# Decode attention over 65,536 keys on one core: engine programs written by hand with their own semaphores, TensorE in a hardware loop, a fixed buffer for each tile

## The chip, the cores and the metric

The kernel runs on one core of a Trainium2 chip. Its time is the device time of one execution in microseconds (us), the median of three runs. The profile comes from one further execution; its times count from the first instruction of the program, and the stretch from there to the last instruction is called the span.

Five engines work side by side, each through its own list of instructions: TensorE (PE, with PEld for its weight loads), VectorE (DVE), ScalarE (ACT), GpSimd (POOL) and SyncE (SP). Here SP does nothing but issue the large loads, ACT issues the load of the queries and the stores. A load is cut over 16 DMA engines, each of which works through its share of the loads in the order in which they were issued; such a list is called a ring below.

## What is computed

One query token with 32 heads attends over 65,536 keys; four query heads share one of eight key/value heads ("a head" below is one of these eight, numbered 0 to 7).

```
B, Hq, Hkv, Sq, Sk, D = 1, 32, 8, 1, 65536, 128      # q, k, v in bf16
k = jnp.repeat(k, rep, axis=1)                        # rep = 4
v = jnp.repeat(v, rep, axis=1)
scores = jnp.einsum("bhqd,bhkd->bhqk", q, k) * scale  # scale = D ** -0.5
p = _softmax(scores, axis=-1)
return jnp.einsum("bhqk,bhkd->bhqd", p, v)
```

Keys and values are 2 x 8 x 65,536 x 128 x 2 bytes = 268.4 MB, each read once. Everything else is small.

## The kernel before

**Tiles.** A head's K and its V come in two tiles each (`s` = 0 and 1, called first and second half), [128 partitions, 256 keys, 128] in bf16, 8.39 MB. A tile lies in one of three buffers of the pool `iopool` (L61, L115), which are handed out in turn: tile n goes where tile n-3 lay, whatever the two hold. The order of the tiles is the order of the loop at L298: K0 first, K0 second, K1 first, V0 first, K1 second, V0 second, K2 first, V1 first and so on; at the end ... K7 second, V6 second, V7 first, V7 second. The very first tile comes in four pieces and the very last in seven (128, 64, 32, 16, 8, 4, 4 keys per partition), so that work can begin early and little is left when the last byte lands.

**Work on a K tile** (`k_step`, L124). DVE transposes the tile in place in four parts (L135); behind each part PE runs 16 matmuls (L141) against the queries, which lie spread out in `wq`. Each half of a tile fills one PSUM bank `sc` with scores, four banks a head; DVE takes each bank's maximum (L148).

**Softmax** (`softmax`, L150). A chain of small steps: maximum over the four banks (L152), a PE transpose (L154), maximum per query head (L156), scaling (L160), a matmul that spreads it (L166), a copy (L168). ACT then computes the exponentials of the four banks (L172) with their sums, and DVE transposes them into `ET` (L181).

**Work on a V tile** (`v_stream`, L187): 64 matmuls (L197) of `ET` against V into `psum_o`. Behind a head's second V tile, `pick` (L205) keeps the right blocks with a mask in four DVE steps (L213, L215), and for each pair of heads `finish` (L231) sums over partitions with a matmul against `sel` (L234), sums the exponentials (L222, L226), inverts (L228) and multiplies (L237). Two stores carry heads 0 to 3 and 4 to 6 away.

**The end** (`finish_last`, L250). The last tile's pieces are used as they land: 48 matmuls of the usual kind for 128 and 64 keys, then 56 that put V on the weight side and give the transposed result `psum_oT` (L282), and eight single ones that give it straight (L268). The transposed part is copied (L286), turned back by a PE transpose (L289), scaled (L292) and added to the straight part (L293); a store follows (L296).

**Order and waits.** The Tile framework lays the five lists out, puts in the semaphores and holds a load back until its buffer's last reader is done. SP's list holds the loads alone, so one that waits holds back all behind it. On PE the scheduler put the matmuls of V6's second half right behind those of K7's second half, ahead of the small softmax matmuls of head 7.

Of the kernel before, what the change touches and what calls it, by code (L numbers as in the profile page):

```python
# [8 lines left out]
ALU = mybir.AluOpType  # L9
ACT = mybir.ActivationFunctionType  # L10
AX = mybir.AxisListType


NT = 256
NB = 128
NW = 16

LATE = (64, 120, 124)
# [3 lines left out]
def kernel(  # L22
# [16 lines left out]

    nc = tc.nc  # L40
# [7 lines left out]
    KT = R // NT  # L48
# [3 lines left out]
    assert W * HPG == 32 and NU == 4 and U == 2  # L52
    SCALE = float(D) ** -0.5

# [3 lines left out]
    const = ctx.enter_context(tc.tile_pool(name="const", bufs=1))  # L58
    opool = ctx.enter_context(tc.tile_pool(name="opool", bufs=1))
    stats = ctx.enter_context(tc.tile_pool(name="stats", bufs=1))  # L60
    iopool = ctx.enter_context(tc.tile_pool(name="iopool", bufs=3))  # L61
    epool = ctx.enter_context(tc.tile_pool(name="epool", bufs=1))
    psc = ctx.enter_context(tc.tile_pool(name="psc", bufs=5, space=bass.MemoryType.PSUM))
    psm = ctx.enter_context(tc.tile_pool(name="psm", bufs=1, space=bass.MemoryType.PSUM))
    pso = ctx.enter_context(tc.tile_pool(name="pso", bufs=2, space=bass.MemoryType.PSUM))


    qn = epool.tile([P, D], bf16, name="qn", tag="E_g")
    for a in range(4):
        nc.scalar.dma_start(out=qn[32 * a:32 * a + 32, :], in_=q[0, :, 0, :])  # L70


    WX = P + 32
    wq = const.tile([P, 4 * WX], bf16)
    nc.vector.memset(wq[:, :], 0.0)
    ident = const.tile([P, P], fp32)
    make_identity(nc, ident[:, :])

    sel = const.tile([P, HPG], fp32)
    nc.vector.tensor_reduce(  # L80
        out=sel[:, :], in_=ident[:, :].rearrange("p (x h) -> p h x", h=HPG), axis=AX.X, op=ALU.max
    )
    blk = const.tile([P, W], fp32)
    nc.vector.tensor_reduce(
        out=blk[:, :], in_=ident[:, :].rearrange("p (j w h) -> p w j h", w=W, h=HPG), axis=AX.XY, op=ALU.max
    )

    mask = const.tile([P, 4], fp32)
    nc.gpsimd.tensor_copy(out=mask[0:64, :], in_=blk[0:64, 0:4])
    nc.gpsimd.tensor_copy(out=mask[64:128, :], in_=blk[64:128, 4:8])  # L90
    one = const.tile([1, 1], fp32)
    nc.gpsimd.memset(one[:, :], 1.0)
    o_out = const.tile([HPG, Hkv - 1, D], bf16)
    lsum_all = const.tile([P, Hkv, NU], fp32)
    qx = const.tile([P, D], bf16)
    nc.vector.transpose(out=qx[:, :].bitcast(fp32), in_=qn[:, :].bitcast(fp32))  # L96

    qv = qx[:, :].rearrange("p (b h r) -> p b r h", b=2, r=2)

    def queries(g):  # L100
        eng = nc.vector if g == 0 else nc.gpsimd
        wv = wq[:, :].rearrange("p (b r x) -> p b r x", b=2, r=2)
        for a in range(4):
            qd = slice(32 * a, 32 * a + 32)
            eng.tensor_copy(  # L105
                out=wv[qd, :, :, 32 * a + 28:32 * a + 28 + HPG],
                in_=qv[qd, :, :, g * HPG:(g + 1) * HPG],
            )

    queries(0)  # L110

    sc_tiles, mx_tiles, ET_tiles, o_tiles, sum_tiles = {}, {}, {}, {}, {}

    def load(x, name, g, s, pieces=(NT,)):
        t = iopool.tile([P, NT, D], bf16, name=name, tag="io", align_bytes=2048)  # L115
        src = x[0, g].rearrange("(p n) d -> p n d", p=P)
        n = 0
        for step in pieces:
            n0 = s * NT + n
            nc.sync.dma_start(out=t[:, n:n + step, :], in_=src[:, n0:n0 + step, :])  # L120
            n += step
        return t

    def k_step(g, s, kn):  # L124
        if s == 0:
            mx_tiles[g] = stats.tile([P, NU], fp32, name="mx4")
        for u in range(U):
            nu = s * U + u
            sc = psc.tile([P, 4 * P], fp32, name="sc")
            sc_tiles[g, nu] = sc  # L130
            for w in range(W):
                n0 = u * NB + w * NW
                if w % 4 == 0:
                    groups = kn[:, n0:n0 + 4 * NW, :].rearrange("p n d -> p (n d)").bitcast(fp32)
                    nc.vector.transpose(out=groups, in_=groups)  # L135
                kv = kn[:, n0:n0 + NW, :].rearrange("p n (b i r) -> p n b i r", b=2, r=2)
                for b in range(2):
                    for r in range(2):
                        bp = 2 * b + r
                        at = bp * WX + 28 - 4 * w  # L140
                        nc.tensor.matmul(  # L141
                            out=sc[:, :],
                            lhsT=wq[:, at:at + P],
                            rhs=kv[:, :, b, :, r],
                            start=(w == 0 and bp == 0),
                            stop=(w == W - 1 and bp == 3),
                        )
            nc.vector.tensor_reduce(out=mx_tiles[g][:, nu:nu + 1], in_=sc[:, :], axis=AX.X, op=ALU.max)  # L148

    def softmax(g):  # L150
        mx = stats.tile([P, 1], fp32, name="mx")
        nc.vector.tensor_reduce(out=mx[:, :], in_=mx_tiles[g][:, :], axis=AX.X, op=ALU.max)  # L152
        psum_t = psm.tile([1, P], fp32, name="psum_t", tag="misc")
        nc.tensor.transpose(out=psum_t[:, :], in_=mx[:, :], identity=ident[:, :])  # L154
        m4 = stats.tile([1, HPG], fp32, name="m4")
        nc.vector.tensor_reduce(  # L156
            out=m4[:, :], in_=psum_t[:, :].rearrange("o (x h) -> o h x", h=HPG), axis=AX.X, op=ALU.max
        )
        mrow = stats.tile([1, P], fp32, name="mrow", tag="row")
        nc.vector.tensor_scalar_mul(  # L160
            out=mrow[:, :].rearrange("o (x h) -> o x h", h=HPG),
            in0=m4[:, :].unsqueeze(1).broadcast_to([1, 32, HPG]),
            scalar1=-SCALE,
        )
        psum_b = psm.tile([P, 1], fp32, name="psum_b", tag="misc")
        nc.tensor.matmul(out=psum_b[:, :], lhsT=mrow[:, :], rhs=one[:, :], start=True, stop=True)  # L166
        nmb = stats.tile([P, 1], fp32, name="nmb")
        nc.vector.tensor_copy(out=nmb[:, :], in_=psum_b[:, :])  # L168

        E_g = epool.tile([P, NU, 4 * P], bf16, name="E_g", tag="E_g")  # L170
        for nu in range(NU):
            nc.scalar.activation(  # L172
                out=E_g[:, nu, :],
                in_=sc_tiles[g, nu][:, :],
                func=ACT.Exp,
                bias=nmb[:, 0:1],
                scale=SCALE,
                accum_out=lsum_all[:, g, nu:nu + 1],
            )
        ET = epool.tile([P, NU, NW, 32], bf16, name="ET")  # L180
        nc.vector.transpose(  # L181
            out=ET[:, :, :, :].rearrange("p s c x -> p (s c x)"),
            in_=E_g[:, :, :].rearrange("p s x -> p (s x)"),
        )
        ET_tiles[g] = ET

    def v_stream(g, s, vb, halves, last):  # L187

        if s == 0:
            o_tiles[g] = pso.tile([P, 4, D], fp32, name="psum_o")  # L190
        for u in range(U):
            vv = vb[:, u * NB:(u + 1) * NB, :].rearrange("p (w c) d -> p w c d", c=NW)
            n = min(2, halves - 2 * u)
            for x in range(n):
                for c in range(NW):
                    j = 2 * x + c % 2
                    nc.tensor.matmul(  # L197
                        out=o_tiles[g][32 * j:32 * j + 32, :, :],
                        lhsT=ET_tiles[g][:, s * U + u, c, :],
                        rhs=vv[:, 4 * x:4 * x + 4, c, :],  # L200
                        start=(s == 0 and u == 0 and c < 2),
                        stop=(last and c >= NW - 2 and 2 * u + x >= halves - 2),
                    )

    def pick(g):  # L205

        if g % 2 == 0 or g == Hkv - 1:
            o_pair = opool.tile([P, 2, D], fp32, name="o_pair")
        else:
            o_pair = sum_tiles[g - 1]  # L210
        sum_tiles[g] = o_pair
        o = o_pair[:, g % 2, :]
        nc.vector.tensor_scalar_mul(out=o, in0=o_tiles[g][:, 0, :], scalar1=mask[:, 0:1])  # L213
        for x in range(1, 4):
            nc.vector.scalar_tensor_tensor(  # L215
                out=o, in0=o_tiles[g][:, x, :], scalar=mask[:, x:x + 1], in1=o, op0=ALU.mult, op1=ALU.add
            )

    def sums(g0, n):

# [131 lines left out]
```

## Time and profile before

| | |
|---|---|
| median of 3 runs | 629.92 us (629.47 to 630.63) |
| profiled execution | 629.52 us, span 627.7 us, granted TensorE clock 0.798 |
| bytes from HBM | 268.47 MB, 428 GB/s over the span |
| PE busy | 346.2 us (55%), 2141 matmuls |
| DVE busy | 339.2 us (54%), 193 instructions |
| ACT busy | 23.6 us (4%) |
| POOL busy | 6.4 us (1%) |
| K turned, L135 | 64 x 4414 ns, 279.0 us |
| K matmuls, L141 | 1024, 260.1 us busy |
| V matmuls, L197 | 1008, 76.6 us busy |

A row of the profile's groups gives the line, the engine, the operation, the busy time of the group, the mean duration of one and the time for which the engine stood idle just before them, with what ended it. An engine's idle time costs nothing by itself; what matters is which work ends last, and whether the DMA engines ever stand still.

### The profile page before, as it was taken

What the parts mean: (1) busy time and instruction counts of PE and PEld (TensorE: products, weight loads), DVE (VectorE), ACT (ScalarE), POOL (GpSimd) and SP (SyncE); (2) the same over time, 40 slices, a digit from 0 to 9 for tenths busy, and PEclk for the clock granted to TensorE, in tenths of its full rate; (3) what the DMA queues carried; (4) which work ended last, traced back from release to release, by engine and by line L of the source; (5) the groups of instructions that cost most, each with busy time, mean ns of one, the idle gap of its engine ahead of it and who ended that gap; (6) DMA issues with size and microseconds to landing.
All of it is one profiled execution on the core that took longest, in us unless ns stands there. A gap on an engine that the chain in (4) does not pass through costs nothing.

```text
span 627.7 us, 4762 instructions
## 1 busy us (share of the span) xinstructions
PE 346.2 (55%) x2141; PEld 145.4 (23%) x2141; DVE 339.2 (54%) x193; ACT 23.6 (4%) x65; POOL 6.4 (1%) x37
## 2 busy tenths in 40 slices
PE   0829582827539084480844808448193581926744
PEld 0313230313214032130311303113041230412312
DVE  3938855739165490654907549074580845709411
ACT  0000100010000100010000010001000001000010
POOL 0000000000000000000000000000000000000000
PEclk9979795967859678596875958758687695876959
DMA  9999999999999999999999999999999999999996
GB/s 369 435 468 402 464 405 460 409 456 413 452 418 448 422 443 427 439 430 435 434 431 439 431 435 434 431 439 427 443 426 444 422 448 418 448 418 452 410 423 281
DMA packets 6161, 268.79 MB, mean 428 GB/s; under 512 B 892, under 2 KB 1148, under 8 KB 1404
## 3 DMA queue, kind: packets, MB, share of 16 engines
q1 hardware_dynamic: 5904, 268.44, 99.0%
q8 instruction: 17, 0.28, 0.2%
q10 hardware_dynamic: 236, 0.04, 0.0%
q14 instruction: 4, 0.03, 0.0%
HBM read 268.47 MB, written 0.01 MB: 428 GB/s over the span
## 4 chain that ended last, share of the span: by engine, by line
DMA 41%; DVE 23%; PE 23%; another core or an unknown queue 11%; ACT 1%; issue 1%; SPq 0%; DVEq 0%; ACTq 0%
DMA kn<-in_k_dram 35%; DVE kn L135 20%; PE sc L141 17%; DMA vb<-in_v_dram 5%; PE psum_o L197 5%; ACT E_g L172 1%; DMA qn<-in_q_dram 1%; DVE o_pair L215 1%; DVE mx L148 1%; DVE ET L181 0%; PE psum_b L166 0%; PE psum_f L234 0%; DVE m L156 0%; PE psum_t L154 0%
## 5 line engine op out<-in xcount | busy, mean ns | idle before, releaser
L141 PE MATMUL sc<-kn,wq 128*128 128x512 bf16 x1024 | 260.1, 415 | 242.9 <-DVE kn L135 242.6
L135 DVE STREAM_TRANSPOSE kn<-kn 128x4096 f32<-128x4096 f32 x64 | 279.0, 4414 | 149.2 <-DMA kn<-in_k_dram 149.2
L141 PEld LDWEIGHTS <-wq 128*128 128x128 bf16 x1024 | 104.9, 103 | 395.9 <-issue 173.2
L197 PE MATMUL psum_o<-vb,ET 128*32 128x512 bf16 x1008 | 76.6, 394 | 11.1 <-DMA vb<-in_v_dram 11.1
L148 DVE TENSOR_REDUCE mx<-sc 128x1 f32<-128x512 f32 x32 | 21.5, 673 | 53.0 <-PE sc L141 53.0
L197 PEld LDWEIGHTS <-ET 128*32 128x32 bf16 x1008 | 34.7, 99 | 50.4 <-issue 19.1
L172 ACT ACTIVATE E_g<-sc,nmb 128x512 bf16<-128x512 f32 x32 | 21.6, 686 | 564.4 <-DVE nmb L168 564.4
L213 DVE TENSOR_SCALAR o_pair<-psum_o,mask 128x128 f32<-128x128 f32 x8 | 2.8, 350 | 49.2 <-PE psum_o L197 49.2
L181 DVE STREAM_TRANSPOSE ET<-E_g 128x2048 bf16<-128x2048 bf16 x8 | 18.4, 2302 | 11.7 <-ACT E_g L172 11.7
L105 POOL COPY wq<-qx 32x16 bf16<-32x16 bf16 x28 | 5.3, 190 | 493.0 <-PE sc L141 491.8
L215 DVE SCALAR_TENSOR_TENSOR o_pair<-psum_o,mask,o_pair 128x128 f32<-128x128 f32 x24 | 8.3, 345 | 0.5
L172 ACT ACTIVATION_READ_ACCUMULATOR E_g<-sc,nmb 128x1 f32 x32 | 6.5, 203 | 0.0
L166 PE MATMUL psum_b<-one,mrow 1*128 1x1 f32 x16 | 2.9, 245 | 5.7 <-DVE mrow L160 5.7
L234 PE MATMUL psum_f<-o_pair,sel 128*4 128x256 f32 (+1 forms) x8 | 2.2, 352 | 6.4 <-DVE o_pair L215 6.4
L96 DVE STREAM_TRANSPOSE qx<-qn 128x64 f32<-128x64 f32 x1 | 0.2, 245 | 9.7 <-DMA qn<-in_q_dram 9.7
L154 PE MATMUL psum_t<-ident,mx 128*1 128x128 f32 x8 | 2.2, 270 | 5.9 <-DVE mx L152 2.9
L222 PE MATMUL psum_l<-lsum_all,sel 128*4 128x8 f32 (+1 forms) x10 | 1.0, 170 | 6.3 <-ACT E_g L172 6.3
L166 PEld LDWEIGHTS psum_b<-one,mrow 1*128 1x128 f32 x16 | 2.4, 186 | 7.0 <-PE psum_t L154 7.0
L156 DVE TENSOR_REDUCE m<-psum_t 1x4 f32<-1x128 f32 x8 | 2.2, 278 | 3.0 <-PE psum_t L154 3.0
L168 DVE COPY nmb<-psum_b 128x1 f32<-128x1 f32 x8 | 1.3, 158 | 4.3 <-PE psum_b L166 4.3
L237 DVE TENSOR_TENSOR o_out<-psum_f,rl 4x256 bf16<-4x256 f32 (+1 forms) x4 | 1.5, 378 | 2.5 <-PE psum_f L234 2.5
L154 PEld LDWEIGHTS psum_t<-ident,mx 128*1 128x1 f32 x8 | 0.6, 79 | 9.6 <-DVE mx L152 4.4
(31 smaller groups left out, 15.7 us busy)
## 6 DMA issues: line engine op xcount, KB each, us to landing
kn<-in_k_dram SPq DMA_DIRECT2D x4, 2048.0 KB, 12.0
vb<-in_v_dram SPq DMA_DIRECT2D x1, 4096.0 KB, 27.1
vb<-in_v_dram SPq DMA_DIRECT2D x1, 2048.0 KB, 31.5
vb<-in_v_dram SPq DMA_DIRECT2D x1, 1024.0 KB
vb<-in_v_dram SPq DMA_DIRECT2D x1, 512.0 KB, 34.3
vb<-in_v_dram SPq DMA_DIRECT2D x1, 256.0 KB, 34.5
vb<-in_v_dram SPq DMA_DIRECT2D x2, 128.0 KB, 26.9
kn<-in_k_dram SPq DMA_DIRECT2D x15, 51.6
```

Source lines behind the costliest of these rows:

```text
L105: eng.tensor_copy(out=wv[qd, :, :, 32 * a + 28:32 * a + 28 + HPG], in_=qv[qd, :, :, g * HPG:(g + 1) * HPG],)
L135: nc.vector.transpose(out=groups, in_=groups)
L141: nc.tensor.matmul(out=sc[:, :], lhsT=wq[:, at:at + P], rhs=kv[:, :, b, :, r], start=(w == 0 and bp == 0), stop=(w == W - 1 and bp == 3),)
L148: nc.vector.tensor_reduce(out=mx_tiles[g][:, nu:nu + 1], in_=sc[:, :], axis=AX.X, op=ALU.max)
L154: nc.tensor.transpose(out=psum_t[:, :], in_=mx[:, :], identity=ident[:, :])
L156: nc.vector.tensor_reduce(out=m4[:, :], in_=psum_t[:, :].rearrange("o (x h) -> o h x", h=HPG), axis=AX.X, op=ALU.max)
L166: nc.tensor.matmul(out=psum_b[:, :], lhsT=mrow[:, :], rhs=one[:, :], start=True, stop=True)
L172: nc.scalar.activation(out=E_g[:, nu, :], in_=sc_tiles[g, nu][:, :], func=ACT.Exp, bias=nmb[:, 0:1], scale=SCALE, accum_out=lsum_all[:, g, ...
L181: nc.vector.transpose(out=ET[:, :, :, :].rearrange("p s c x -> p (s c x)"), in_=E_g[:, :, :].rearrange("p s x -> p (s x)"),)
L197: nc.tensor.matmul(out=o_tiles[g][32 * j:32 * j + 32, :, :], lhsT=ET_tiles[g][:, s * U + u, c, :], rhs=vv[:, 4 * x:4 * x + 4, c, :], start ...
L213: nc.vector.tensor_scalar_mul(out=o, in0=o_tiles[g][:, 0, :], scalar1=mask[:, 0:1])
L215: nc.vector.scalar_tensor_tensor(out=o, in0=o_tiles[g][:, x, :], scalar=mask[:, x:x + 1], in1=o, op0=ALU.mult, op1=ALU.add)
```

## The change

Only the schedule, the buffers and the handling of sums change; tile sizes and the large matmuls and transposes stay.

- The kernel writes each engine's list itself inside one critical section, with some twenty semaphores of its own. The engines meet once more at its start and at its end.
- The three buffers are fixed: `A` for first halves of K, `Bb` for second halves of K, `C` for all V tiles. The seven pieces of V7's second half go into `A`. The order of the loads stays as it was. SP waits for the reader of the buffer ahead of each load (L131 to L142).
- PE runs its steps for heads 1 to 7 with the values of heads 0 to 6 as a loop of seven passes (L381); ahead of it stand K0 and its softmax, behind it V7. Inside a pass the order is: K first half, V first half, K second half, softmax matmuls (`maxima`), V second half, sum. Semaphores that PE waits for are counted down again (`take`).
- On DVE, `bank_max(0)` stands between the third and the fourth part of a tile in all heads, and `ET` of a head is made after `pick` of the head before.
- The sums of the exponentials become a 129th column of `o_sb` (L240), so that one matmul of 4 x 129 gives result and sum of a head (L392); each head is finished by itself (L282, L284). `mask` is made on DVE, ahead of the first K tile, instead of on POOL. At the end the transposed part is added by a product with the identity into the same PSUM bank as the straight part (L427), in place of transpose, scaling and addition.

```diff
+    io = [sb(f"io{b}", [P, NT, D], bf16, 2048) for b in "ABC"]
...
+    section = tc.tile_critical()
+    ctx.enter_context(section)
+
+    sy = nc.sync
+    for i in range(4):
+        n0 = i * NT // 4
+        sy.dma_start(out=A[:, n0:n0 + NT // 4, :], in_=k_src[0][:, n0:n0 + NT // 4, :]).then_inc(s_part[i], 16)
+    sy.dma_start(out=Bb[:, :, :], in_=k_src[0][:, NT:R, :]).then_inc(s_kb, 16)
+    for g in range(1, Hkv):
+        sy.wait_ge(s_bank, NU * (g - 1) + U)
+        sy.dma_start(out=A[:, :, :], in_=k_src[g][:, 0:NT, :]).then_inc(s_ka, 16)
+        if g > 1:
+            sy.wait_ge(s_vd, 2 * (g - 1))
+        sy.dma_start(out=C[:, :, :], in_=v_src[g - 1][:, 0:NT, :]).then_inc(s_v, 16)
+        sy.wait_ge(s_bank, NU * g)
+        sy.dma_start(out=Bb[:, :, :], in_=k_src[g][:, NT:R, :]).then_inc(s_kb, 16)
+        sy.wait_ge(s_vd, 2 * (g - 1) + 1)
+        sy.dma_start(out=C[:, :, :], in_=v_src[g - 1][:, NT:R, :]).then_inc(s_v, 16)
+    sy.wait_ge(s_vd, 2 * L)
+    sy.dma_start(out=C[:, :, :], in_=v_src[L][:, 0:NT, :]).then_inc(s_v, 16)
+    sy.wait_ge(s_bank, NU * L + U)
+    n = 0
+    for i, step in enumerate(PARTS):
+        sy.dma_start(out=A[:, n:n + step, :], in_=v_src[L][:, NT + n:NT + n + step, :]).then_inc(s_late[i], 16)
+        n += step
...
+    for g in range(Hkv):
+        turn_k(g, 0)
+        at = turn_k(g, 1)
+        ve.wait_ge(s_d, at)
+        ve.tensor_reduce(out=mx[:, :], in_=mx4[:, :], axis=AX.X, op=ALU.max).then_inc(s_m, 1)
...
+        if g > 0:
+            pick(g - 1)
+        ve.wait_ge(s_x, g + 1)
...
+        ve.transpose(
+            out=ET[:, :, :, :].rearrange("p s c x -> p (s c x)"), in_=E_g[:, :, :].rearrange("p s x -> p (s x)")
+        ).then_inc(s_et, 1)
+        if g > 0:
+            after_pe()
+            at = done(ve.reciprocal(out=rl[:, :], in_=psum_f[:, D:D + 1]))
+            ve.wait_ge(s_d, at)
+            ve.tensor_scalar_mul(out=o_out[:, g - 1, :], in0=psum_f[:, 0:D], scalar1=rl[:, 0:1]).then_inc(s_o, 1)
...
+    def take(s, n=1):
+        te.wait_ge(s, n).then_inc(s, -n)
...
+    def maxima():
+        take(s_m)
+        te.transpose(out=psum_t[:, :], in_=mx[:, :], identity=ident[:, :]).then_inc(s_pe, 1)
+        take(s_m)
+        te.matmul(out=psum_b[:, :], lhsT=mrow[:, :], rhs=one[:, :], start=True, stop=True).then_inc(s_pe, 1)
...
+    k_tile(0)
+    k_tile(1)
+    maxima()
+
+    with nc.Fori(0, L, 1, engines=(PE,)):
+        take(s_et)
+        take(s_wq, 4)
+        k_tile(0)
+        take(s_v, 16)
+        v_tile(0, C)
+        k_tile(1)
+        maxima()
+        take(s_v, 16)
+        v_tile(1, C)
+        take(s_pick)
+        te.matmul(out=psum_f[:, :], lhsT=sel[:, :], rhs=o_sb[:, :], start=True, stop=True).then_inc(s_pe, 1)
+
+    take(s_et)
+    te.matmul(out=psum_b[0:HPG, :], lhsT=sel[:, :], rhs=lcol[:, :], start=True, stop=True).then_inc(s_pe, 1)
+    take(s_v, 16)
+    v_tile(0, C)
+    v_tile(1, A, 3)
...
+    single(n2, n3)
+    take(s_m)
+    te.matmul(out=psum_l, lhsT=oT[:, :], rhs=ident[:, :], start=False, stop=False)
+    single(n3, NB).then_inc(s_pe, 1)
```

`s_bank` counts finished score banks (four a head), `s_vd` finished V tiles (two a head, raised by the tile's last matmul), `L` is 7. `k_tile(s)` is the 64 matmuls of one K tile with a `take(s_k)` ahead of each 16; `v_tile(s, t)` the 64 of one V tile.

## The prediction

> **What bounds the kernel now.** I looked first at the page's slices and queues, to see whether any engine or the transfers are full.
>
> ```profile
> DMA  9999999999999999999999999999999999999996
> ...
> q1 hardware_dynamic: 5904, 268.44, 99.0%
> q8 instruction: 17, 0.28, 0.2%
> ```
>
> The load queue fills 99.0% of the 16 DMA engines' time, and no slice but the last is below 9 tenths; PE and DVE are at 55% and 54%. The trace's single packets say the same: a ring moves 64 KB in 2.418 us, an 8.39 MB tile lands every 19.32 us, and between 3 and 620 us no ring rests. So the time is a start, 268.4 MB at full rate, and an end; nothing on the other engines counts unless it makes the rings run dry. Whether that can happen is read from SP's timeline, which says when a load enters the rings (start us, duration):
>
> ```profile
> 476.17 0.33 SPq L120 DMA_DIRECT2D kn<-in_k_dram  x1
> 510.19 0.33 SPq L120 DMA_DIRECT2D vb<-in_v_dram  x1
> 514.68 0.33 SPq L120 DMA_DIRECT2D kn<-in_k_dram  x1
> 548.95 56.39 SPq L120 DMA_DIRECT2D vb<-in_v_dram  x9
> ```
>
> These are K7 first, V6 first, K7 second, and then V6 second with all of V7. K7 second entered at 514.68 and had landed at 566.46: two tiles always lie ahead of the one issued. The third view is the chain of waits around the same place (start us, us, what), with one earlier head for the softmax steps:
>
> ```profile
> 122.51 0.70 DVE mx L148
> ...
> 124.42 0.35 PE psum_b L166 x2
> 124.77 3.63 PE psum_o L197 x57
> ...
> 435.39 5.20 PE psum_o L197 x55
> ...
> 510.16 4.50 PE psum_o L197 x64
> ...
> 566.46 17.43 DVE kn L135 x4
> 583.89 0.04 issue
> 583.93 3.66 PE sc L141 x16
> 587.59 0.02 issue
> 587.61 0.33 SPq L120
> ...
> 624.59 0.22 PE psum_t L289
> 624.80 0.03 issue
> 624.83 0.35 DVE o_t L292
> ...
> 625.27 0.34 DVE o_out L293
> ```
>
> A landed K tile takes 17.43 us of DVE and 3.66 of PE, the softmax steps up to L166 2.26 us (122.51 to 124.77), a V tile 4.50 us of PE.
>
> **The change, part by part.** *1. The order of loads against the fixed buffers (L131 to L142).* In the middle this costs nothing. If a first K half lands at 0, V first lands at 19.3, K second at 38.6, V second at 57.9, the next at 77.3. K first is used up at 17.43 + 0.65 (`bank_max(0)`) + 3.66 = 21.8, V first at 26.3; the load that needs C then has to enter by 38.6 less the 2.1 us below: 10 us spare. K second is used up at 60.4, its softmax steps end at 62.6, V second at 67.1; needed by 75.2: 8 us spare. DVE's `pick` and `ET` behind it (0.1 + 4 x 0.35 + 2.31) end at 71 and the next K first lands at 77.3, so the later `ET` is covered too; without that cover it would push the next K tile by 4 us.
>
> At the end the order has no K tile between V6 second and V7 first, and both lie in C. `sy.wait_ge(s_vd, 14)` (L140) stands ahead of all eight remaining loads, 8.39 MB and the seven pieces, although A has long been free. That wait ends when V6's second half is used up, and PE reaches that only behind K7's second half and its softmax matmuls: 566.46 + 17.43 + 0.65 + 0.04 + 3.66 + 2.26 + 4.50 + 0.05 = 595.0. The restart of empty rings: the first load was issued at 0.74, its first packet starts at 1.75, and its 2.1 MB were down by 7.35 to 7.88, which is 4.84 us at full rate behind 2.5 to 3.0. I take 2.1 us from issue to full flow (bounds 1.0 and 2.3). So V7 flows from 597.1. Before, the slowest ring passed from V6 to V7 at 585.3. **Gap: 11.8 us**, and it is bare: behind it the same bytes, the same pieces and the same end follow. PE's clock is a bound: 64 matmuls behind the softmax steps took 4.5 us at 124.77 and 6.1 at 435.39, where windows show a granted clock of 0.50; +1.6 at most.
> [...]
>
> *2. The first head.* Here K0 second and K1 first are neighbours. K0 second lands at 42.23 and is used up at 64.0; softmax to L168 66.6, four exponentials 2.8, `ET` 2.31: 71.8 (before, one part of K1 was turned in that hole). K1 first then takes to 93.6, V0 first to 98.1. V0 second enters there, and the load ahead of it, K1 second, ran out at 99.3 on the first ring and 100.95 on the last. With 2.1 us of restart the last ring is dry for nothing; bounds 0 and +1.5; I take 0.
>
> *3. The loop.* PE's program now is some 600 recorded instructions, about 1170 with the weight loads, against 4282 profiled. Before, the profile shows 17 instruction packets, one for each 250 instructions. In the packet records each holds its ring up by 1.35 us (a ring's landing went from 60.8 to 62.3 behind the first), and they go round eight rings, so these are 2.7 us late by the end: 563.0 against 566.0 for K7 second. If the program's 4.6 blocks come once, no ring has more than one: **-1.35 us**. Bounds: -2.7 (none) and 0 (one packet for each 250 executed, since about as many are executed as before). The jump back itself falls where PE waits anyway: in the terms of part 1 the sum matmul ends about 69.5 and the next K tile's first part is turned at 77.3 + 4.4 = 81.7, so 12 us hide it.
>
> *4. DVE and POOL.* Per head a 0.1 us sum is added and the small steps lose their partners; DVE stands idle 17 us ahead of K7's second half alone, and 149.2 us in all before L135 for DMA. Making `mask` ahead of the first tile delays it by 0.3 us, and A's next load enters at 35.7 instead of 35.4, needed by 39. Both nothing.
>
> *5. The end.* Before: transpose 0.27, o_t 0.35, o_out 0.34. Now an f32 product (two passes, 0.38 as at L275), four single matmuls and one 0.35 step. The singles run behind it instead of beside o_t; that gives 0 (bounds -0.3 and +0.2).
>
> *6. Entry and exit.* One more meeting of the engines at each end. The span's last DMA ends at 626.5 and the span at 627.7, so such a meeting is under 1.2 us. I take 0.3 together (bounds 0 and 1.0).
>
> Sum: 11.8 - 1.35 + 0.3 = +10.75 on the profiled execution's span of 627.7, with 1.8 us around it: 629.52 + 10.75 = 640.3. That execution lies 0.4 below the median of the runs, so **640.7 us**.
>
> **The rivals.** *A. Instructions come late or often.* The jump back makes PE fetch its loop again, seven times three blocks, and always on the same rings: 7 x 1.35 = 9.5 us lateness instead of 2.7, that is +6.8 against before and +8.1 against my term: 649. For it: 17 packets show that PE's code does not stay, and that each costs a ring 1.35 us. Against: they went round eight rings evenly. [...]
> [...]
>
> *B. The first head runs dry.* If K1 first is late by more than I count, all rings wait at 99 to 101 and every later landing shifts. A shift of 4 us (another 3 us of late `ET` and a V tile at half clock) gives 644.7, still in the range; more than that, 647.
>
> *C. The gap is hidden and the loop pays: faster.* If V6 second were used up before the rings run dry, the wait at L140 would cost nothing, and the saved packets would remain: 629.9 - 2.7 + 0.3 = 627.5. It decides when V7 first enters by about 583, which needs 12 us less between K7's landing and L140's release. Nothing in the 28.5 us chain (17.43 of it one DVE row of fixed length) can give that; only PE taking V6 ahead of K7 would, and its list does not.
>
> **How the numbers follow.** My forecast 0.82, A 0.08, B beyond the range 0.04, C 0.05; the rest is the gap closing to nothing just so. The low end takes parts 1, 3, 5 and 6 at their cheap ends: 640.7 - 1.1 - 1.35 - 0.3 - 0.3 = 637.6, and 0.3 for the scatter of the runs: 637.3. The high end takes the dear ones: +1.6 clock, +1.5 first head, +1.35 packets, +0.7 meetings: 645.9, written as 646. A lies above. A change under 0.2% (1.3 us) could not be told from none; slower by more 0.95, within 0.01, faster 0.04.
>
> **What would show it.** In the new profile SP's wait at L140 should end at about 594, on PE L367; the DMA row should have a slice of 3 to 5 tenths near 590, and nowhere else before the end; K7's second half should reach DVE at about 565. Fewer than six packets on the instruction queue would bear out part 3; some 25 or more would be A. A V0 second that starts late, a dip near 100 us, would be B. A DMA row without a dip would make the prediction wrong, as would any PE wait inside a pass that no semaphore of DVE or DMA explains.

## The result, and the profile after

The changed kernel takes 647.65 us (median of 6 runs, 647.21 to 653.07) against 629.78 us before: the ratio of the runs' means is 1.0293, 95% interval 1.026 to 1.0327. The forecast was 640.7 us in 637.3 to 646.0. The kernel did become slower, and for the reason that the forecast gave, but by 17.9 us where it had 10.8, which is above its range. One execution of the six took 653.07; none of its kind was profiled, and why it was longer stays open. The profiled execution took 647.41 us with a span of 645.6.

The page's slices and queues come first again:

```profile
DMA  8999999999999999999999999999999999991896
GB/s 362 480 394 455 455 391 391 455 391 451 451 398 455 447 402 451 447 418 434 451 426 422 451 439 410 451 447 402 451 447 402 455 443 402 451 447 77 366 414 261
...
q1 hardware_dynamic: 5904, 268.44, 96.4%
q8 instruction: 4, 0.07, 0.0%
```

One slice of 40, from 581 to 597 us, has fallen to 1 tenth and 77 GB/s, and the next to 8; from the second slice up to these all stand at 9. The load queue's share fell from 99.0% to 96.4%. Four instruction packets are left of 17. SP's timeline and its own waits say which load is late:

```profile
100.28 0.33 SPq L139 DMA_DIRECT2D ioC<-in_v_dram  x1
...
521.60 0.43 SPq L137 DMA_DIRECT2D ioB<-in_k_dram  x1
555.30 0.33 SPq L139 DMA_DIRECT2D ioC<-in_v_dram  x1
599.37 0.33 SPq L141 DMA_DIRECT2D ioC<-in_v_dram  x1
599.75 3.48 SPq L145 DMA_DIRECT2D ioA<-in_v_dram  x7
```

```profile
SPq L139 <- PE psum_o L367: 241.9, 7, 36.1
SPq L135 <- PE psum_o L367: 237.9, 6, 41.3
SPq L141 <- PE psum_o L367: 43.7, 1, 43.7
```

V7's first half (L141) enters at 599.37, when PE has used up V6's second half. The packet records show the rings done with V6 between 585.0 and 586.8, and V7's first half down at 620.90. Its transfer at full rate takes 19.34 us, so on the slowest ring it is as if full flow began at 601.56: 14.7 us are lost there, 13.5 of them without a byte (to 600.34) and the rest in a slow start. The waits at L139 and L135 are longer in all, but apart from the one that ends at 100.28 each ends at least 5 us before the load ahead of it begins to land (the one that ends at 555.30 some 10 us before K7's second half does, at 565.7), so in these waits the rings did not run dry, and the waiting cost nothing. The timeline of the stretch ahead of 599.37 (start us, us, what; idle time before it in brackets):

```profile
567.98 13.10 DVE L223 STREAM_TRANSPOSE ioB<-ioB 128x4096 f32<-128x4096 f32 x3 [16.47 <-DMA ioB<-in_k_dram]
...
581.98 0.69 DVE L210 TENSOR_REDUCE mx<-sc 128x1 f32<-128x512 f32 x1 [0.91 <-PE sc L343]
582.59 4.43 DVE L223 STREAM_TRANSPOSE ioB<-ioB 128x4096 f32<-128x4096 f32 x1
...
587.17 3.64 PE L343 MATMUL sc<-ioB,wq 128*128 128x512 bf16 x16 [1.74 <-PEq L328]
...
590.85 0.69 DVE L210 TENSOR_REDUCE mx<-sc 128x1 f32<-128x512 f32 x1 [3.83 <-PE sc L343]
...
593.14 6.20 PE L367 MATMUL psum_o<-ioC,ET 128*32 128x512 bf16 x64
```

Two things here were not in the forecast's chain. DVE stands idle for 0.91 us ahead of the first bank's maximum, because PE is not yet done with that bank; and the V tile takes 6.20 us, not 4.50. Windows over the last piece show the granted clock (the column behind POOL's):

```profile
590.50:593.00 2.50, 0.72 (x5) 0.25 (x3) 1.34 (x4) 0.00 (x0) 0.00 (x0) 1.00 0.00 0
593.00:595.00 2.00, 2.00 (x22) 1.02 (x26) 0.16 (x1) 1.56 (x5) 0.00 (x0) 0.81 0.00 0
595.00:597.00 2.00, 2.00 (x24) 0.80 (x18) 0.00 (x0) 1.22 (x4) 0.00 (x0) 0.50 0.00 0
```

The trace's clock records have it at half from 594.25 to 597.66, so the fall comes 1.1 us into the V tile; the last two columns show the rings at rest.

The chain of waits, the third view that was shown of the kernel before, is short in this kernel: it reaches back only 5 us from the last instruction, since PE's waits on counted-down semaphores are put down to its own sequencer (PEq; 233.8 us at L343). What it holds can be set against the end of the kernel before:

```profile
640.51 0.38 PE sc L421 x2
640.89 0.69 PE sc L423 x24
641.58 0.32 PE sc L415 x4
...
641.92 0.50 PE sc L427 x2
642.42 0.44 PE sc L415 x4
...
642.89 0.34 DVE o_out L294
```

From the end of L423 (641.58) to the end of the last DVE step (643.23) are 1.65 us, against 1.36 before (624.25 to 625.61). The granted clock from 641.9 to 643.0 is 0.56; at the same place of the kernel before (624.2 to 625.2) it is 1.00.

### The profile page after: what moved, and what is told of

Read it like the earlier page. It is cut to its first block, busy times and chain, and to the rows that moved or that the text cites. A ratio compares the mean times of both kernels' runs of the same rounds, so it can differ in the third digit from the quotient of the medians.

```text
span 645.6 us, 4822 instructions
## 1 busy us (share of the span) xinstructions
PE 357.0 (55%) x2140; PEld 146.2 (23%) x2140; DVE 342.6 (53%) x203; ACT 23.6 (4%) x65; POOL 6.0 (1%) x35
## 3 DMA queue, kind: packets, MB, share of 16 engines
q1 hardware_dynamic: 5904, 268.44, 96.4%
## 5 line engine op out<-in xcount | busy, mean ns | idle before, releaser
L343 PE MATMUL sc<-ioB,wq 128*128 128x512 bf16 x512 | 130.3, 416 | 128.7 <-PEq L328 128.7
L223 DVE STREAM_TRANSPOSE ioB<-ioB 128x4096 f32<-128x4096 f32 x32 | 140.3, 4421 | 103.8 <-DMA ioB<-in_k_dram 103.8
L343 PE MATMUL sc<-ioA,wq 128*128 128x512 bf16 x512 | 130.6, 416 | 105.1 <-PEq L328 105.1
L223 DVE STREAM_TRANSPOSE ioA<-ioA 128x4096 f32<-128x4096 f32 x32 | 140.2, 4420 | 24.0 <-DMA ioA<-in_k_dram 23.9
L343 PEld LDWEIGHTS sc<-ioB,wq 128*128 128x128 bf16 x512 | 51.7, 103 | 207.2 <-issue 159.3
L343 PEld LDWEIGHTS sc<-ioA,wq 128*128 128x128 bf16 x512 | 51.6, 103 | 182.0 <-issue 134.4
L367 PE MATMUL psum_o<-ioC,ET 128*32 128x512 bf16 x960 | 79.9, 433 | 17.8 <-PEq L328 17.8
L367 PEld LDWEIGHTS psum_o<-ioC,ET 128*32 128x32 bf16 x960 | 34.4, 106 | 59.1 <-issue 36.1
L240 DVE TENSOR_REDUCE o_sb<-lsum 128x1 f32<-128x4 f32 x7 | 1.1, 156 | 40.2 <-PE psum_o L367 40.2
L392 PE MATMUL psum_f<-o_sb,sel 128*4 128x129 f32 x14 | 2.7, 271 | 12.3 <-PEq L328 12.3
L367 PE MATMUL psum_o<-ioA,ET 128*32 128x512 bf16 x48 | 6.1, 485 | 5.1 <-DMA ioA<-in_v_dram 5.1
L246 DVE SCALAR_TENSOR_TENSOR o_sb<-psum_o,mask,o_sb 128x128 f32<-128x128 f32 x24 | 8.4, 351 | 0.8
L392 PEld LDWEIGHTS psum_f<-o_sb,sel 128*4 128x4 f32 x14 | 0.8, 83 | 15.6 <-issue 15.6
```

Of the source, the lines that this page charges most:

```text
L223: ve.transpose(out=x, in_=x).then_inc(s_k, 1)
L246: ins = ve.scalar_tensor_tensor(out=o, in0=psum_o[:, x, :], scalar=mask[:, x:x + 1], in1=o, op0=ALU.mult, op1=ALU.add)
L343: ins = te.matmul(out=sc[nu][:, :], lhsT=wq[:, at:at + P], rhs=kv[:, :, b, :, r], start=(w == 0 and bp == 0), stop=(w == W - 1 and bp == 3),)
L367: ins = te.matmul(out=psum_o[32 * j:32 * j + 32, :, :], lhsT=ET[:, s * U + u, c, :], rhs=vv[:, 4 * x:4 * x + 4, c, :], start=(s == 0 and u ...
L392: te.matmul(out=psum_f[:, :], lhsT=sel[:, :], rhs=o_sb[:, :], start=True, stop=True).then_inc(s_pe, 1)
```

## The experiments

All start from the changed kernel, 647.65 us. Theory 1 is that the rings run dry, at L140 and a little in the first head; theory 2 is that the loop on PE costs the time; theory 3 that the transfers themselves are slower.

**1. A and C exchanged at the end.**

```diff
-    sy.wait_ge(s_vd, 2 * L)
-    sy.dma_start(out=C[:, :, :], in_=v_src[L][:, 0:NT, :]).then_inc(s_v, 16)
     sy.wait_ge(s_bank, NU * L + U)
+    sy.dma_start(out=A[:, :, :], in_=v_src[L][:, 0:NT, :]).then_inc(s_v7, 16)
+    sy.wait_ge(s_vd, 2 * L)
...
-        sy.dma_start(out=A[:, n:n + step, :], in_=v_src[L][:, NT + n:NT + n + step, :]).then_inc(s_late[i], 16)
+        sy.dma_start(out=C[:, n:n + step, :], in_=v_src[L][:, NT + n:NT + n + step, :]).then_inc(s_late[i], 16)
```

(V7's first half gets a semaphore of its own, and PE reads V7's halves from the buffers in which they now lie.)

> V7's first half goes into A, which is free by then, and the seven pieces into C; the order of the loads stays. Theory 1 (the wait at L140 leaves all rings dry, 14.7 us from 586.8 to 601.6 in the changed kernel's packet records): the dip vanishes and the time falls by about that, to 632.5 (631.5 to 634.0). Theory 2 (the PE loop is what costs: instruction fetches stall PE or hold rings up): the loop is untouched, so the time stays above 643. Theory 3 (the fixed buffers make the transfers themselves slower): the dip goes but tiles land further apart than 19.32 us, 638 or more.

632.71 us (630.0 to 634.51, 10 runs). The page's slices:

```profile
DMA  8999999999999999999999999999999999999996
```

The dip is gone and with it 14.9 us, the 14.7 of the packet records. Tiles land 19.32 us apart in both kernels. The gap is shown, and theories 2 and 3 are out as the main cause of the loss. The kernel before took 630.08 us in the same rounds, so 2.6 us are left for the other experiments.

**2. The loop written out.**

```diff
-    with nc.Fori(0, L, 1, engines=(PE,)):
+    for _ in range(L):
```

> The loop on PE is written out seven times, nothing else. Theory 1: schedule and gap stay; 17 instruction packets instead of 4, two on a ring instead of one, so 648.5 (647.0 to 650.0). Theory 2: the jumps back are gone and the time falls by several us, below 644.

648.47 us (646.79 to 649.96, 4 runs). The page's queues:

```profile
q8 instruction: 17, 0.28, 0.2%
```

17 packets are back. K7's second half lands over 3.25 us from the first ring to the last (567.22 to 570.47), against 1.8 us with the loop (565.71 to 567.52) and 3.0 before. So a packet does hold up its ring, and the loop spares that; the time differs by 0.8, less than the runs scatter. Theory 2 falls: the loop costs nothing that can be seen.

**3. V's second half ahead of the softmax matmuls.**

```diff
         k_tile(1)
-        maxima()
         take(s_v, 16)
         v_tile(1, C)
+        maxima()
```

> In the loop PE takes V's second half ahead of the softmax matmuls. Theory 1: L140 is released earlier by the softmax chain (2.36 us) and by the half clock that PE falls to behind it (6.20 instead of 4.55 us, 1.65): 643.6 (642.8 to 645.2), and the V tile at about 4.55 us. Rival (the clock falls because of what lies ahead of the softmax chain, the waits inside the K tile): 6.2 us stays and the time is 645.3. Theory 2: no change, 647 to 648.

642.53 us (641.84 to 644.1, 4 runs): 5.1 us less, where 4.05 were expected. The timeline of the same stretch:

```profile
585.83 3.64 PE L343 MATMUL sc<-ioB,wq 128*128 128x512 bf16 x16 [1.74 <-PEq L328]
...
589.41 4.55 PE L367 MATMUL psum_o<-ioC,ET 128*32 128x512 bf16 x64
...
594.00 0.33 SPq L141 DMA_DIRECT2D ioC<-in_v_dram  x1
```

The V tile takes 4.55 us although the 1.74 us of waiting in the K tile are still there; so do all seven second halves, of which six had taken 6.2 us in the changed kernel. From DVE's start on K7's second half to L141 are 26.97 us instead of 31.39, and the rings' rest is 10.4 us. The rival, that the waits inside the K tile slow the clock by themselves, falls. But the softmax matmuls ahead of a V tile do not make it dear every time: six times of seven in the changed kernel, three of seven in experiment 4, and 31 of 49 over the seven profiles (the changed kernel's and those of the other six experiments) that keep this order.

**4. The first bank's maximum behind the fourth part.**

```diff
-                if u == 1 and h == 0:
+                if u == 1 and h == 0 and g == 0 and s == 0:
                     bank_max(0)
+        if g or s:
+            bank_max(0)
         return bank_max(1)
```

> The maximum of a tile's first bank stands behind the fourth transposed part instead of ahead of it (not for the very first tile). Theory 1: DVE no longer waits there for PE (0.9 us a tile). That is hidden in the middle, but V0 second enters 1.9 us earlier (98.4 instead of 100.28), so that the dry stretch at 100 us shrinks from about 2 us to under 0.6, and the chain ahead of L140 is 0.9 shorter: 645.0 (644.3 to 646.3). Rival (the late landings behind the first head have another cause, and DVE has time to spare): 647 to 648.

642.85 us (642.39 to 643.11, 4 runs): 4.8 us less, where 2.65 were expected. The timeline:

```profile
565.61 17.42 DVE L223 STREAM_TRANSPOSE ioB<-ioB 128x4096 f32<-128x4096 f32 x4 [16.75 <-DMA ioB<-in_k_dram]
...
582.95 0.65 DVE L210 TENSOR_REDUCE mx<-sc 128x1 f32<-128x512 f32 x1
586.86 0.69 DVE L210 TENSOR_REDUCE mx<-sc 128x1 f32<-128x512 f32 x1 [3.25 <-PE sc L345]
```

The expectation took away the wait alone. But behind the fourth part the 0.65 us of the maximum itself also lie beside PE's last 16 matmuls: 21.2 us from DVE's start to the second bank's end, against 22.8, so 1.6 us a tile. It counts twice in the first head: V0 second entered at 97.06 instead of 100.28, the records show no dry stretch there, and K7's second half had landed on all rings at 565.2 instead of 567.5. It counts once more ahead of L140: the gap is 13.1 us instead of 14.7.

**5. The first head alone.** One part of K1 is transposed ahead of `ET` of head 0, as in the kernel before.

```diff
+        if g == 0:
+            turn_k(1, 0, 0)
         ve.wait_ge(s_x, g + 1)
```

(`turn_k(1, 0, 0)` does that one part; the later call leaves it out.)

> One part of K1's first tile is transposed ahead of ET of head 0, as in the kernel before; nothing else changes. Theory (the rings also run dry at about 100 us because V0 second enters too late): V0 second enters some 4 us earlier, the dry stretch there (1.5 us as a mean over the rings) is gone, every later landing comes about 1.5 to 2.2 us earlier, the gap at L140 stays: 645.8 (645.0 to 646.6). Rival (the later landings come from the start of the kernel or from the instruction packets): 647 to 648.

645.41 us (644.46 to 653.1, 4 runs), inside the theory's range. SP's timeline:

```profile
97.39 0.33 SPq L139 DMA_DIRECT2D ioC<-in_v_dram  x1
```

V0 second enters 2.9 us earlier, where some 4 were expected, and the rings' mean rest around 100 us falls from 1.5 to 0.1. K7's second half lands 1.9 us earlier on the slowest ring (565.64 for 567.52) and 1.4 in the mean over the rings. The gap at the end is 13.9 us in this profile, so of the 2.2 us in the time some 0.8 may be the gap's.

**6. Exchange and later maximum together.** The edits of 1 and 4.

> The exchange of A and C at the end and the later bank maximum together. Theory: both dry stretches are gone, so what is left against the kernel before is the start (+0.2), the end and exit (+0.7) and less lateness of the slowest ring (-0.8 at K7's second half): 630.0 (629.3 to 630.8). Rival (the two do not add, since both repair the same 2 us): 632.5.

630.26 us (629.08 to 632.46, 12 runs), ratio to the kernel before 0.9998 (0.998 to 1.0015).

```profile
DMA  8999999999999999999999999999999999999996
```

The packet records have no dry stretch between 5 and 620 us. The two repairs do add.

**7. The same with the old end.**

```diff
-    te.matmul(out=psum_l, lhsT=oT[:, :], rhs=ident[:, :], start=False, stop=False)
+    te.transpose(out=psum_f[:, 0:D], in_=oT[:, :], identity=ident[:, :]).then_inc(s_pe, 1)
...
+    at = done(ve.tensor_scalar_mul(out=o_t, in0=psum_f[:, 0:D], scalar1=rl7[:, 0:1]))
+    after_pe()
+    ve.wait_ge(s_d, at)
+    ve.scalar_tensor_tensor(
+        out=o_out[:, L, :], in0=sc[2][0:HPG, 0:D], scalar=rl7[:, 0:1], in1=o_t, op0=ALU.mult, op1=ALU.add
+    ).then_inc(s_o, 1)
```

> As e6, and the end as in the kernel before: the transposed part is turned back by a PE transpose, scaled and added on DVE instead of by the product with the identity. Theory (the f32 product stands in the way of the last four matmuls, +0.3 in the profile from the last L423 to the end of the last DVE step): 0.3 below e6, 629.7. Rival (one DVE step less is worth as much as the second f32 pass): the same as e6 within 0.2.

630.58 us (629.29 to 632.38, 11 runs), not below experiment 6: the rival holds. The two chains of waits, of experiment 6 and then of this one, say why:

```profile
622.84 0.72 PE sc L425 x24
...
624.55 0.34 DVE o_out L296
```

```profile
625.75 0.69 PE sc L431 x24
...
627.53 0.34 DVE o_out L300
```

From the last of the 24 to the last DVE step's end are 1.33 us with the product and 1.43 with the old end. The 1.65 in the changed kernel's profile, at a clock of 0.56, was that execution's own: with the same end, experiments 1 and 5 take 1.32 and 1.33 at a clock of 1.00.

No version beat the kernel before; experiment 6 equals it.

## Why the prediction was wrong in size, step by step

The sum on the slowest ring, from the packet records and the two spans, is closed: K7's second half lands 1.51 us later (566.01, 567.52); the gap takes 14.72 (586.84 to 601.56); from V7's first half to the last byte it takes 0.94 more (20.52 for 19.58); from the last byte to the end 0.76 more (4.18 for 3.42). That is 17.93, and the spans differ by 17.9. The forecast had 10.75. Of the 7.2 us between them, 2.9 lie in the gap, 2.9 ahead of it (the start, the first head and the packets), 0.9 in the last tile and 0.5 at the ends.

*Part 1, the gap: the mechanism was right, the size was not.* 11.8 were forecast and 14.7 came. The step that failed is "566.46 + 17.43 + 0.65 + 0.04 + 3.66 + 2.26 + 4.50", the chain from DVE's start on K7's second half to the end of L140's wait: it has 28.6 us, and 31.4 came. Of the 2.8 us more, 0.9 are a wait that it left out and 1.7 are the V tile.
The chain priced `bank_max(0)` by its own 0.65 us and not by what it waits for. In the kernel before it stood behind the fourth part, where PE had filled the bank at 583.59, and its row has no idle time:

```profile
579.48 4.40 DVE L135 STREAM_TRANSPOSE kn<-kn 128x4096 f32<-128x4096 f32 x1
...
583.80 0.65 DVE L148 TENSOR_REDUCE mx<-sc 128x1 f32<-128x512 f32 x1
```

Between the third and the fourth part it waits 0.91 us for PE. Experiment 4 puts the whole price of the new place, these 0.65 included, at 1.6 us a tile. And 4.50 for the V tile was the cheap end of a price whose dear end the prediction itself names as a bound, +1.6; 6.20 came, and experiment 3 takes these 1.65 us away.
In the trace's clock records the half clock that makes the tile dear lasts 3.41 us, from 594.25 to 597.66; in the 3.41 us ahead of it PE was busy for 1.66.
Why one tile is hit and another is not, the runs do not settle. Behind the softmax matmuls 31 tiles of 49 are dear, and the last pass is in six of the seven profiles, so the cheap end was the less likely one; in the rows that the prediction had, one of three was dear.
The restart was right: 2.1 us taken, 2.2 measured (599.37 to 601.56). So was the statement that nothing is lost in the middle: no slice between 120 and 580 us is below 9 tenths.

*Part 2, the first head: taken as 0, was about 2.* V0 second entered at 100.28 and not at 98.1, for the same unpriced wait, twice. K7's second half reached DVE at 567.98 and not at about 565. Experiment 5 takes most of the loss away by itself: 1.9 us at K7's landing on the slowest ring. This is rival B in kind, though not in its size.

*Part 3, the packets: right as far as it went.* The rings lie 1.8 us apart at K7's second half, not 3.0: 1.2 us gained where 1.35 were taken. But the fourth packet falls at 630.1 into the last tile, on rings that the restart had brought within 0.6 us of each other: one ring finished the 64-key piece at 636.38, the next at 635.45. That is the size of the 0.94 above.
Rival A did not come. PE's instruction packets (q8 in the page's queues) stand at 82.9, 99.7, 131.0 and 630.1 in the records, while the loop jumped back six times with about 535 instructions a pass, so none came between 131.0 and 630.1, where the passes from the second to the last ran. The 1.74 us in which PE waits inside the K tile are no wait for instructions: they end 0.15 us behind DVE's fourth part (587.02, 587.17), and in experiment 4 they are gone.

*Part 4* was right that `mask` costs nothing (A's next load entered at 35.19, before at 35.36), and overlooked that DVE's order, not its load, is what changed. *Part 5* held: experiment 7 finds nothing to gain. *Part 6* took 0.3 for both ends; the first packet starts 0.2 later (1.95 for 1.75) and from the last store's landing to the end there are 0.3 more (644.1 to 645.6, 626.5 to 627.7). Another 0.3 of the 0.76 behind the last byte lie in the chain at the end, 1.65 us at a clock of 0.56 for 1.36 at 1.00.

Rival C fell, as expected: experiment 1 shows what it would have needed, a load that may enter before V6 is used up. The range failed because its dear end added single bounds from rows of the kernel before, and the wait that the new order makes was in none of them. Its last chances also do not follow from the ones ahead of them, which make slower 0.94 and faster 0.05.

## What to carry to other kernels

A kernel whose rings are full is judged by asking, for each load, what must be done before it may enter and how long after that the rings still have work; here six waits at L135, 237.9 us in all, cost nothing, and one of 43.7 us at L141, behind which the rings ran dry, cost 14.7. Count buffers where the pattern of loads ends as well as in its middle: one buffer that took two tiles in a row turned a hidden chain into a bare one (14.9 us in experiment 1). And where an instruction changes its place, price what it waits for there, not only itself (here 0.65 us for itself and 1.6 with the wait); that price came back in every stretch that lay bare (three times, 4.8 us in experiment 4).

## What the hardware showed that was not expected

- One 16 KB instruction packet (0.88 to 0.97 us in the records of the two kernels) holds the ring on which it falls up by some 1.35 us, and the 14 that had come by K7's second half put the rings of the kernel before 3 us apart, against 1.8 us behind three packets in the changed kernel. DVE began on K7's second half only behind the slowest ring (565.71 to 567.52 on the rings, 567.98 on DVE), so code length shows in the landing of data; in the time, experiment 2 does not show it clear of the runs' scatter.
- From the issue of a load into empty rings to full flow took 2.2 us (599.37 to 601.56), to its first packet about 1.0 (600.34).
- Behind a stretch of some 2.3 us with two small matmuls in it the 64 matmuls of a V tile were dear in 31 of 49 cases; in the changed kernel's clock records PE's clock is at half for 3.41 us in each of its six, and the tile takes 6.20 us instead of 4.55. Where the V tile came directly behind the K tile, none was dear: 4.55 us in all seven first halves of the changed kernel and in all seven second halves of experiment 3.
